# Choosing ScalarE or VectorE for PSUM copies by an estimate of both queues, packing the first chunk's score batches, and loading one x block by itself

## Chip, cores, metric

The kernel runs on one core of a Trainium2 chip. The metric is the device time of one execution in microseconds; the median of several executions is quoted, of "fast" runs alone. Ratios are computed as the mean time of one kernel's fast runs over that of the other's fast runs of the same rounds, so they are not quite the ratio of the medians that stand beside them.

## The reference

A layer normalisation feeds two branches, and the input is added to their sum:

```python
xn = layernorm(x)                        # S = 2048 rows, D = 512, bf16
qkv = xn @ wqkv                          # 32 heads of 16
scores = q @ k.T * 16**-0.5              # a query sees itself and the 255 keys before it
attn = softmax(masked scores) @ v @ wo
glu = ((xn @ w_gate) * (xn @ w_up)) @ w_down     # F = 1792
out = x + attn + glu
```

## The kernel before

The kernel works on four chunks of 512 rows. For each chunk and each group `c` of 8 heads it makes batches of scores, one exponential per batch, masks, and a values product. The dense matmuls (projections, gate, up, down, output) are "fillers" that are put between the batches by a count of cost units, one unit being about one 512-column matmul. The order of instructions on each engine is fixed when the program is built.

First, a chunk gets its tiles, and GpSimd writes the constants that V needs (ones in columns 16 and 17 of each head, which later give the softmax sums):

```python
def new_chunk(self, T):
    ...                                   # Q, K, Ko, V, VS tiles
    nc.gpsimd.memset(self.heads(self.V[T])[:, :, :, 16:18], 1.0)
    nc.gpsimd.memset(self.V[T][:, VW - 16:], 0.0)
    nc.gpsimd.memset(self.VS[T][:, SW - 16:], 0.0)
```

The copies out of PSUM, the memory (in banks) that TensorE writes its results to. V always goes to ScalarE and fills columns 0 to 15 of each head. K, Q and the gate go to ScalarE only when 11 units have passed since the last score batch (`act_free`), otherwise to VectorE:

```python
def proj_v(self, t, ks=range(4)):
    ...                                   # 4 matmuls into one PSUM bank
    nc.scalar.activation(out=self.heads(self.V[T])[:, b]...[:, :, :, 0:16], in_=ps..., func=ACT.Copy)

# in gate(); proj_qk() is alike
    if self.act_free:
        nc.scalar.activation(out=self.gsb[:], in_=ps[:], func=ACT.Copy)
    else:
        nc.vector.tensor_copy(out=self.gsb[:], in_=ps[:])
```

A batch of scores. There is one score tile of four banks (`bufs=1`), so the next batch can start only when the exponential has read the last one. GpSimd then cuts the far edge of the window with "triangles", two for each place:

```python
def scores(self, T, c, pieces):
    S = self.s_tiles.tile([128, 4, 512], F32, tag="S", name="S")
    ...                                   # 16 or 24 packed matmuls (32x64 tiles of the array)
    nc.scalar.activation(out=P[:, :, 0:col], in_=S[:, :, 0:col], func=ACT.Exp, scale=0.25)
    for at in self.places(pieces, 4):
        for half in (slice(0, 64), slice(64, 128)):
            self.triangle(P[half, :, at:at + 64], False)      # gpsimd.affine_select
```

```python
def project(T):
    add(0, lambda: self.new_chunk(T))
    for b in range(4):
        for ks in halves:
            add(2, lambda t=4 * T + b, ks=ks: self.proj_v(t, ks), self.first[T, 0])
    add(0, lambda: self.swap_halves(T, self.nc.sync), self.first[T, 0])
    ...                                   # Q and K projections
```

All other PSUM tiles, dense products and values sums alike, share a ring of four banks (`ps_m`).

The softmax here doesn't subtract the row's maximum and nothing guards it: scores larger than these inputs give would overflow.

## Time and profile before

| | before |
|---|---|
| median time | 269.14 us (3 runs; 268.98 us over the 4 runs known later) |
| span in the profile | 267.5 us |
| TensorE busy | 258.4 us (97%) |
| VectorE, ScalarE, GpSimd busy | 181.7, 170.6, 113.8 us |

The page of the kernel before gives busy time and share for each engine, and further down the chain that ended last, by engine:

```profile
span 267.5 us, 8861 instructions
...
PE 258.4 (97%) x3860; PEld 119.1 (45%) x3882; DVE 181.7 (68%) x352; ACT 170.6 (64%) x132; POOL 113.8 (43%) x281
...
PE 88%; DVE 7%; issue 1%; DMA 1%; ACT 1%; SPq 0%; POOL 0%; DVEq 0%; POOLq 0%
```

TensorE (PE) is busy nearly always and holds 88% of the chain. Busy time of matmuls can hide stalls, because the recorded ends are modelled. The starts are safer: count the dense matmuls between two score batches, allow 0.216 us for each, 0.45 us for the batch and, where a values sum falls between, 0.97 us (first chunk) or 1.27 us (later), and compare with the distance of the two batches' starts. (22 matmul records are missing from this trace, 3860 against 3882 weight loads.) What a distance has above its allowance is called a hole below. In this kernel all distances fit within 0.1 us but three, which hold 0.18, 0.31 and 0.15 us more.

The timeline of the kernel before, at the start (start us, duration us, engine, line, what; in brackets the idle time before it and who ended it):

```profile
2.86 0.69 DVE L148 BATCH_NORM_STATS2 st<-x 128x6 f32<-128x512 bf16 x1 [1.02 <-DMA x<-in_A_x_dram]
...
4.80 0.70 DVE L148 BATCH_NORM_STATS2 st<-x 128x6 f32<-128x512 bf16 x1 [0.84 <-DMA x<-in_A_x_dram]
...
14.43 0.28 PE L261 MATMUL S<-Q,K 16*64 16x192 bf16 x4
```

The second block's statistics wait for the load of three blocks at once, and the first scores come at 14.43 us.

### The profile page before, as it was taken

What the parts mean: (1) busy time and instruction counts of PE and PEld (TensorE: products, weight loads), DVE (VectorE), ACT (ScalarE), POOL (GpSimd) and SP (SyncE); (2) the same over time, 40 slices, a digit from 0 to 9 for tenths busy, and PEclk for the clock granted to TensorE, in tenths of its full rate; (3) what the DMA queues carried; (4) which work ended last, traced back from release to release, by engine and by line L of the source; (5) the groups of instructions that cost most, each with busy time, mean ns of one, the idle gap of its engine ahead of it and who ended that gap; (6) DMA issues with size and microseconds to landing.
All of it is one profiled execution on the core that took longest, in us unless ns stands there. A gap on an engine that the chain in (4) does not pass through costs nothing.

```text
span 267.5 us, 8861 instructions
## 1 busy us (share of the span) xinstructions
PE 258.4 (97%) x3860; PEld 119.1 (45%) x3882; DVE 181.7 (68%) x352; ACT 170.6 (64%) x132; POOL 113.8 (43%) x281
## 2 busy tenths in 40 slices
PE   6899999999999999999999999999999999999994
PEld 6444434444444444444444444444444444434453
DVE  4377898958756859676674868857762575978251
ACT  2675658696556776769656676668765667665500
POOL 5215333422674533345556433545444353443500
PEclk9999999999999999999999999999999999999999
DMA  6999911120023000001014100000200010000002
GB/s 205 373 358 334 250 22 22 23 47 0 4 61 81 20 2 4 2 2 44 5 23 97 43 0 5 0 4 2 44 5 20 26 39 2 2 0 2 4 2 81
DMA packets 19336, 15.13 MB, mean 57 GB/s; under 512 B 7264, under 2 KB 19296, under 8 KB 19296
## 3 DMA queue, kind: packets, MB, share of 16 engines
q1 hardware_dynamic: 18464, 14.09, 18.1%
q8 instruction: 30, 0.49, 0.7%
q10 hardware_dynamic: 832, 0.46, 0.6%
q14 instruction: 10, 0.08, 0.1%
HBM read 9.70 MB, written 2.10 MB: 44 GB/s over the span
## 4 chain that ended last, share of the span: by engine, by line
PE 88%; DVE 7%; issue 1%; DMA 1%; ACT 1%; SPq 0%; POOL 0%; DVEq 0%; POOLq 0%
PE up L359 17%; PE gp L345 17%; PE psd L378 16%; PE qkp L212 11%; PE S L261 9%; PE acc L316 6%; PE psd L384 5%; PE vp L200 4%; PE L L378 2%; DMA x<-in_A_x_dram 1%; DVE hT L363 1%; DVE st L148 1%; DVE at L322 1%; DVE gsb L353 1%; DVE xn L168 1%
## 5 line engine op out<-in xcount | busy, mean ns | idle before, releaser
L268 ACT ACTIVATE P<-S 128x2048 bf16<-128x2048 f32 x76 | 141.0, 1855 | 57.4 <-PE S L261 49.9
L137 POOL TENSOR_SCALAR_AFFINE_SELECT P<-P 64x256 bf16<-64x256 bf16 x224 | 97.3, 434 | 128.9 <-ACT P L268 118.2
L345 PE MATMUL gp<-xnT,Wg 128*128 128x512 bf16 x224 | 60.0, 380 | 0.1
L359 PE MATMUL up<-xnT,Wu 128*128 128x512 bf16 x224 | 59.6, 380 | 0.0
L378 PE MATMUL psd<-Wd,hT 128*128 128x512 bf16 (+1 forms) x198 | 48.7, 368 | 1.4 <-issue 1.3
L363 DVE TENSOR_TENSOR hT<-up,gsb 128x512 bf16<-128x512 f32 x56 | 38.4, 686 | 16.0 <-PE up L359 14.4
L289 DVE TENSOR_TENSOR P<-P,diag 128x512 bf16<-128x512 bf16 (+1 forms) x76 | 30.6, 404 | 10.4 <-ACT P L268 10.4
L322 DVE STREAM_TRANSPOSE at<-acc 128x512 f32<-128x512 f32 x30 | 19.7, 695 | 19.7 <-PE acc L316 19.7
L378 PEld LDWEIGHTS <-hT 128*128 128x128 bf16 x238 | 21.6, 98 | 25.3 <-issue 2.6
L359 PEld LDWEIGHTS <-Wu 128*128 128x128 bf16 x224 | 20.4, 98 | 25.3 <-issue 2.5
L345 PEld LDWEIGHTS <-Wg 128*128 128x128 bf16 x224 | 20.3, 98 | 25.5 <-issue 2.7
L261 PE MATMUL S<-Q,K 16*64 16x320 bf16 (+1 forms) x720 | 31.2, 260 | 0.4
L261 PE MATMUL S<-Q,Ko 32*64 32x320 bf16 (+1 forms) x720 | 31.1, 260 | 0.0
L212 PE MATMUL qkp<-xnT,Wqkv 128*128 128x512 bf16 x128 | 30.0, 380 | 0.0
L261 PEld LDWEIGHTS <-K 16*64 16x64 bf16 x720 | 12.2, 103 | 32.2 <-issue 32.2
L353 DVE CAST gsb<-gp 128x512 bf16<-128x512 f32 x36 | 24.5, 681 | 2.6 <-PE gp L345 1.3
L351 ACT ACTIVATE gsb<-gp 128x512 bf16<-128x512 f32 x20 | 11.9, 597 | 11.8 <-PE gp L345 11.1
L316 PE MATMUL acc<-P,VS 64*32 64x320 bf16 (+4 forms) x672 | 18.9, 254 | 0.0
L316 PE MATMUL acc<-P,V 64*32 64x320 bf16 (+4 forms) x672 | 18.4, 254 | 0.1
L212 PEld LDWEIGHTS <-Wqkv 128*128 128x128 bf16 x128 | 11.7, 98 | 14.5 <-issue 1.4
L384 PE MATMUL psd<-Wo,OT 128*128 128x512 bf16 (+1 forms) x55 | 15.5, 368 | 0.6 <-issue 0.6
L316 PEld LDWEIGHTS <-V 64*32 64x32 bf16 x720 | 14.5, 90 | 2.8 <-issue 2.4
(55 smaller groups left out, 194.1 us busy)
## 6 DMA issues: line engine op xcount, KB each, us to landing
Wg<-in_B_w_gate_dram SPq DMA_DIRECT2D x2, 896.0 KB, 10.4
Wu<-in_B_w_up_dram SPq DMA_DIRECT2D x2, 896.0 KB, 13.0
Wd<-in_B_w_down_dram SPq DMA_DIRECT2D x1, 1792.0 KB, 17.3
out_dram<-y SPq DMA_DIRECT2D x14, 128.0 KB, 1.8
Wqkv<-in_A_wqkv_dram SPq DMA_DIRECT2D x3, 512.0 KB, 6.4
x<-in_A_x_dram SPq DMA_DIRECT2D x1, 1024.0 KB, 10.9
VS<-V SPq DMA_DIRECT2D x6, 144.0 KB, 2.6
x<-in_A_x_dram SPq DMA_DIRECT2D x1, 512.0 KB, 11.4
```

The lines of the kernel that those rows point to most:

```text
L137: nc.gpsimd.affine_select(out=v, in_=v, pattern=pattern + [[1 if diag else -1, 64]], compare_op=ALU.is_ge if diag else ALU.is_gt, fill=0.0 ...
L212: nc.tensor.matmul(ps[:], lhsT=self.Wqkv[:, k, lo:lo + 128], rhs=self.xnT[T][:, :, k, :], start=(k == 0), stop=(k == 3))
L261: nc.tensor.matmul(S[64 * par:64 * par + 64, e, col:col + n], lhsT=(self.Ko if par else self.K)[U][rows, c, keys], rhs=self.Q[T][rows, c, ...
L268: nc.scalar.activation(out=P[:, :, 0:col], in_=S[:, :, 0:col], func=ACT.Exp, scale=0.25)
L289: self.nc.vector.tensor_tensor(out=v, in0=v, op=ALU.min, in1=self.diag.unsqueeze(1).unsqueeze(1).to_broadcast([128, 4, n, 64]))
L316: nc.tensor.matmul(accs[par][32 * e:32 * e + 32, q:q + n], lhsT=v, rhs=P[rows, e, col:col + n], start=(i == 0), stop=(i == len(todo) - 1), ...
L345: nc.tensor.matmul(ps[:], lhsT=self.Wg[:, k, 128 * f:128 * f + 128], rhs=self.xnT[T][:, :, k, :], start=(k == 0), stop=(k == 3))
L353: nc.vector.tensor_copy(out=self.gsb[:], in_=ps[:])
L359: nc.tensor.matmul(ps[:], lhsT=self.Wu[:, k, 128 * f:128 * f + 128], rhs=self.xnT[T][:, :, k, :], start=(k == 0), stop=(k == 3))
L363: nc.vector.tensor_tensor(out=self.hT[T][:, f, :], in0=ps[:], in1=self.gsb[:], op=ALU.mult)
L378: nc.tensor.matmul(ps, lhsT=self.hT[T][:, f, 128 * b:128 * b + 128], rhs=self.Wd[:, f, c0:c1], start=(f == 0), stop=False)
L384: self.nc.tensor.matmul(ps, lhsT=self.OT[T][:, c, 128 * b:128 * b + 128], rhs=self.Wo[:, c, c0:c1], start=False, stop=(c == 3))
```

## The change

The intent is to keep both copying engines' queues short, to save one score batch, and to start earlier:

- Every copy goes to the engine that an estimate says will finish it first. The estimate books, in cost units, what has been given to ScalarE and VectorE.
- The first chunk's 16 batches (four of them with 384 columns) become 15 of 512, some shared by two head groups. The cost constants that place the work go from 1.85 and 5.5 to 1.9 and 6.0.
- x is loaded as blocks 0, 1 and 2 to 3 instead of 0 and 1 to 3.
- At the end one store moves from ScalarE to VectorE, and the identity matmul that added x for it goes.

```diff
+REST = (((0, *SIX), (1, *SIX), (0, *FOUR)), ((1, *FOUR), (2, *FOUR)), ((2, *SIX), (3, *SIX), (3, *FOUR)))
+SCORES, VALUES = 1.9, 6.0
+COPY = dict(act=2.8, dve=3.2)
+EXP, MASK, HALF, SUMS, DIVIDE, TURN, STATS = 8.7, 1.9, 1.7, 4.2, 8.2, 6.1, 4.2
@@ loads
-        for lo, hi in ((0, 1), (1, 4)):
+        for lo, hi in ((0, 1), (1, 2), (2, 4)):
@@ copies
+    def book(self, engine, took, ready=0):
+        self.free[engine] = max(self.free[engine], self.now, ready) + took
+    def copy(self, out, in_, engine=None):
+        if engine is None:
+            engine = min(COPY, key=lambda e: max(self.free[e], self.now) + COPY[e])
+        self.book(engine, COPY[engine])
+        if engine == "act":
+            nc.scalar.activation(out=out, in_=in_, func=ACT.Copy)
+        else:
+            nc.vector.tensor_copy(out=out, in_=in_)
@@ proj_v (proj_qk and gate alike)
-        nc.scalar.activation(out=self.heads(self.V[T])[:, b]..., in_=ps..., func=ACT.Copy)
+        self.copy(self.heads(self.V[T])[:, b]..., ps..., engine)
@@ batches
+            out += [tuple((c, *p) for p in pieces) for pieces in (LATER if T else SHARED)]
+            if T == 0 and c < 3:
+                out.append(REST[c])
@@ tail
-            if b in (1, 3):
-                add(1, lambda b=b: self.add_x(T, b, 0 if b == 1 else 1))
+        add(1, lambda: self.add_x(T, 3, 1))
-            self.store(T, b, on_act=(b == 1))
+            self.store(T, b)
```

More of the change, by code (lines that the diff above doesn't have):

```diff
@@ L18 @@
 SW = 4 * 16 * 18 + 16
-FIRST = (((5, 5, 7), (0, 0, 4)), ((3, 3, 5), (1, 1, 5)),
-         ((3, 6, 7), (7, 7, 7), (2, 2, 6)), ((4, 4, 7), (6, 6, 7)))
+SHARED = ((5, 5, 7), (0, 0, 4)), ((3, 3, 5), (1, 1, 5)), ((3, 6, 7), (7, 7, 7), (2, 2, 6))
+FOUR, SIX = (4, 4, 7), (6, 6, 7)
 LATER = (((-2, 0, 2), (0, 0, 4)), ((5, 5, 7), (1, 1, 5)), ((-3, 0, 1), (7, 7, 7), (3, 3, 7)),
          ((-4, 0, 0), (6, 6, 7), (2, 2, 6)), ((-1, 0, 3), (4, 4, 7)))
-ACT_FREE = 11
+REST = (((0, *SIX), (1, *SIX), (0, *FOUR)), ((1, *FOUR), (2, *FOUR)), ((2, *SIX), (3, *SIX), (3, *FOUR)))
+SCORES, VALUES = 1.9, 6.0
+COPY = dict(act=2.8, dve=3.2)
+EXP, MASK, HALF, SUMS, DIVIDE, TURN, STATS = 8.7, 1.9, 1.7, 4.2, 8.2, 6.1, 4.2
 class Kernel:
@@ L107, in setup @@
         self.K, self.Ko, self.V, self.VS = {}, {}, {}, {}
-        self.strips, self.at = {}, {}
+        self.strips, self.parts, self.at = {}, {}, {}
     def new_chunk(self, T):
@@ L149, in norm_stats @@
         nc.vector.bn_aggr(out=self.mv[:, t % n, :], in_=st[:])
+        self.book("dve", STATS)
         self.stats[t] = [self.mv, t % n, None]
@@ L169, in norm_apply @@
                                 scalar2=rs[:, j:j + 1], op0=ALU.subtract, op1=ALU.mult)
+        self.book("dve", MASK)
         self.xns[t] = xn
@@ L193, in bank, with proj_v @@
         return self.cur
-    def proj_v(self, t, ks=range(4)):
+    def book(self, engine, took, ready=0):
+        self.free[engine] = max(self.free[engine], self.now, ready) + took
+    def copy(self, out, in_, engine=None):
+        nc = self.nc
+        if engine is None:
[5 more added lines that the diff above has]
+            nc.vector.tensor_copy(out=out, in_=in_)
+    def proj_v(self, t, ks=range(4), engine=None):
         nc = self.nc
@@ L203, in proj_v, with proj_qk @@
             return
-        nc.scalar.activation(out=self.heads(self.V[T])[:, b].rearrange("p (r g) d -> p r g d", r=2)[:, :, :, 0:16],
-                             in_=ps.rearrange("p (g r d) -> p r g d", g=16, r=2), func=ACT.Copy)
-    def proj_qk(self, T, c, is_k, ks=range(4), on_act=False):
+        self.copy(self.heads(self.V[T])[:, b].rearrange("p (r g) d -> p r g d", r=2)[:, :, :, 0:16],
+                  ps.rearrange("p (g r d) -> p r g d", g=16, r=2), engine)
+    def proj_qk(self, T, c, is_k, ks=range(4), engine=None):
         nc = self.nc
@@ L215, in proj_qk @@
             return
+        self.copy((self.K if is_k else self.Q)[T][:, c, :], ps[:], engine)
         if is_k:
-            if self.act_free:
-                nc.scalar.activation(out=self.K[T][:, c, :], in_=ps[:], func=ACT.Copy)
-            else:
-                nc.vector.tensor_copy(out=self.K[T][:, c, :], in_=ps[:])
             nc.vector.tensor_scalar(out=self.Ko[T][:, c, :], in0=self.K[T][:, c, :],
                                     scalar1=self.odd[:, 0:1], scalar2=None, op0=ALU.mult)
-        elif on_act or self.act_free:
-            nc.scalar.activation(out=self.Q[T][:, c, :], in_=ps[:], func=ACT.Copy)
-        else:
-            nc.vector.tensor_copy(out=self.Q[T][:, c, :], in_=ps[:])
+            self.book("dve", HALF)
     def first_chunk(self):
@@ L242, in first_chunk, with batches, scores @@
                 self.norm_transpose(b + 1, False)
-            self.proj_v(b)
-        self.proj_qk(0, 0, 1)
-        self.proj_qk(0, 0, 0, on_act=True)
+            self.proj_v(b, engine="act")
+        self.proj_qk(0, 0, 1, engine="dve")
+        self.proj_qk(0, 0, 0, engine="act")
         self.swap_halves(0, self.nc.scalar)
-        self.proj_qk(0, 1, 1)
-    def scores(self, T, c, pieces):
+        self.proj_qk(0, 1, 1, engine="dve")
+    def batches(self, T):
+        out = []
+        for c in range(4):
+            out += [tuple((c, *p) for p in pieces) for pieces in (LATER if T else SHARED)]
+            if T == 0 and c < 3:
+                out.append(REST[c])
+        return out
+    def scores(self, T, pieces):
         nc = self.nc
         S = self.s_tiles.tile([128, 4, 512], F32, tag="S", name="S")
+        P = self.ppool.tile([128, 4, 512], BF16, tag="P", name="P")
         col = 0
-        for m, q0, q1 in pieces:
+        for c, m, q0, q1 in pieces:
             U, j = divmod(8 * T + m, 8)
@@ L265, in scores @@
                                      skip_group_check=True)
+            self.parts.setdefault((T, c), []).append((P, col, m, q, n))
             col += n
-        P = self.ppool.tile([128, 4, 512], BF16, tag="P", name="P")
         nc.scalar.activation(out=P[:, :, 0:col], in_=S[:, :, 0:col], func=ACT.Exp, scale=0.25)
-        self.strips[(T, c, pieces)] = P
+        self.book("act", EXP)
+        self.masked = self.free["act"]
+        self.strips[(T, pieces)] = P
         for at in self.places(pieces, 4):
@@ L276, in places @@
         out, at = [], 0
-        for m, q0, q1 in pieces:
+        for _, m, q0, q1 in pieces:
             out += [at + 64 * (q - q0) for q in range(q0, q1 + 1) if q == m + far]
@@ L280, in places, with mask_diag @@
         return out
-    def mask_diag(self, T, c, pieces):
-        P = self.strips[(T, c, pieces)]
+    def mask_diag(self, T, pieces):
+        P = self.strips.pop((T, pieces))
         places = [at // 64 for at in self.places(pieces, 0)]
-        step = places[1] - places[0] if len(places) == 2 else 1
+        n = len(places)
+        step = places[1] - places[0] if n > 1 else 1
+        assert places == list(range(places[0], places[-1] + 1, step))
         v = P.rearrange("p e (b x) -> p e b x", x=64)[:, :, places[0]:places[-1] + 1:step, :]
-        n = len(places)
         self.nc.vector.tensor_tensor(out=v, in0=v, op=ALU.min,
                                      in1=self.diag.unsqueeze(1).unsqueeze(1).to_broadcast([128, 4, n, 64]))
+        self.book("dve", MASK, self.masked)
     def values(self, T, c, accs=None):
@@ L297, in values @@
             accs = [self.ps_m.tile([128, 512], F32, tag="M", name="acc") for _ in range(2)]
-        todo = []
-        for pieces in LATER if T else FIRST:
-            P, col = self.strips.pop((T, c, pieces)), 0
-            for m, q0, q1 in pieces:
-                todo.append((P, col, m, 64 * q0, 64 * (q1 - q0 + 1)))
-                col += 64 * (q1 - q0 + 1)
+        todo = self.parts.pop((T, c))
         for i, (P, col, m, q, n) in enumerate(todo):
@@ L322, in values @@
             nc.vector.transpose(out=at[:, par].rearrange("p b r -> p (b r)"), in_=accs[par][:])
+        self.book("dve", TURN)
         self.at[(T, c)] = at
@@ L335, in divide @@
                                 in1=rz.unsqueeze(3).to_broadcast([128, 2, 16, 16]), op=ALU.mult)
+        self.book("dve", DIVIDE)
         nc.vector.transpose(out=self.OT[T][:, c, :], in_=on.rearrange("p b r d -> p (b r d)"))
@@ L349, in gate @@
         self.gsb = self.work.tile([128, 512], BF16, tag="gsb", name="gsb")
-        if self.act_free:
-            nc.scalar.activation(out=self.gsb[:], in_=ps[:], func=ACT.Copy)
-        else:
-            nc.vector.tensor_copy(out=self.gsb[:], in_=ps[:])
+        self.copy(self.gsb[:], ps[:])
     def up(self, T, f, ks):
@@ L363, in up @@
         nc.vector.tensor_tensor(out=self.hT[T][:, f, :], in0=ps[:], in1=self.gsb[:], op=ALU.mult)
+        self.book("dve", COPY["dve"])
     def down(self, T, b, lo, hi):
@@ L402, in store @@
             nc.vector.tensor_tensor(out=y, in0=ps, in1=self.x[:, t, c0:c1], op=ALU.add)
+            self.book("dve", COPY["dve"])
         (nc.scalar if on_act else nc.sync).dma_start(out=self.out_d[128 * t:128 * t + 128, c0:c1], in_=y)
@@ L489, in run @@
         self.xns, self.stats, self.sums = {}, {}, {}
-        self.act_free = False
+        self.now, self.free = 0, dict(act=0, dve=0)
         self.setup()
@@ L496, in run @@
         for T in range(NCH):
-            for c in range(4):
-                self.first[T, c] = len(steps)
-                for pieces in LATER if T else FIRST:
+            for pieces in self.batches(T):
+                for c, *_ in pieces:
+                    self.first.setdefault((T, c), len(steps))
                     self.last[T, c] = len(steps)
-                    steps.append((T, c, pieces))
+                steps.append((T, pieces))
         due = {g: key for key, g in self.last.items()}
-        SCORES, VALUES = 1.85, 5.5
         self.beside = {}
@@ L506, in run @@
         total = sum(w[0] for w in work) - RESERVE + SCORES * len(steps) + VALUES * (len(due) - 1)
-        spent, n, scored = 0, 0, 0
+        spent, n = 0, 0
+        self.free = dict(act=0, dve=0)
         valued, ready = -1, -1
@@ L518, in fill @@
                     break
-                self.act_free = spent + cost - scored >= ACT_FREE
+                spent += cost
+                self.now = spent
                 f()
-                spent += cost
                 n += 1
@@ L527, in values @@
                 return False
+            spent += VALUES
+            self.now = spent
             self.values(*due[g])
-            spent += VALUES
             return True
@@ L539, in run @@
             valued = ready
+            spent += SCORES
+            self.now = spent
             self.scores(*s)
-            scored = spent
-            spent += SCORES
             upto = total * (g + 1) / len(steps)
```

## The prediction

> **What bounds the kernel now.** TensorE, almost without a hole. The page gives it 258.4 us busy of 267.5 (97%), granted clock 1.00; the chain of waits is 88% PE. "Busy" could hide stalls, so I read the distances between starts in the timeline: back-to-back 512-column matmuls start every 0.216 us in every stage, also where VectorE is fullest (9.75 of 10 us at 30 to 40 us, windows view). A score batch costs 0.45 us between the neighbouring matmuls, a values group 1.2 to 1.3 us, the same everywhere. From 8.4 to 263.8 us I find about 0.25 us of stall that is not a missing record (36.6 to 37.2 us). VectorE (182 us busy) and ScalarE (171 us) wait for PE far more than PE for them.
>
> **What the change does.**
> 1. Copies. In the built order ScalarE's gate copies go from 20 to 34, Q and K from 11 to 16, V from 16 to 10; VectorE's from 36 to 22, 21 to 16, 0 to 6. At 0.60 us (ScalarE) and 0.68 us (VectorE) VectorE loses about 8 us with the moved store, ScalarE gains 7. The Trainium skill ("TensorEngine Tiling (Array Packing)", PSUM Bottleneck) advises both engines for PSUM evacuation; but in this trace evacuation hardly stalls PE: worth 0.2 us. Risk: a copy behind a 1.88 us exponential keeps a bank, and the product waiting for it blocks VectorE. A gate bank is needed again some 2.6 us later, so I expect little of that.
> 2. First chunk: 15 batches of 512 columns for 12 of 512 and 4 of 384. Matmuls and columns stay; one entry and exit of the packed mode goes. The same page (Key Properties) says a mode switch drains TensorE; the trace has about 0.09 us before each batch. 16 batches take about 7.0 us, 15 about 6.75: 0.2 us of PE.
> 3. x block 1 alone. The start is critical: VectorE's second statistics begin at 4.80 us, when the 384 KB load lands (3.5 us after issue; the 128 KB load took 2.0). Alone, block 1 should land near 3.3 us and those statistics begin near 3.97 us. The chain from there (statistics, scale, transposes) moves 0.8 us earlier, up to PE at 8.43 us. Weight loads are issued about 0.45 us later (V's landed at 6.2 us, first use would be near 6.65), and the warm-up matmuls end at 5.67 us: I count 0.7 us.
> 4. Tail: one identity matmul (0.22 us) goes; its store moves to VectorE, which has room. Last bank to end unchanged (263.8 to 267.5 us).
>
> **Sum.** 0.7 + 0.2 + 0.2 + 0.2, all on the critical path, less perhaps 0.1 for new waits: about 1.3 us. From 269.1: **267.8 us**, range 267.0 to 269.0. Faster by over 2%: 0.01; within 2%: 0.97; slower by over 2%: 0.02.
>
> **What would show it.** Step 3: second statistics at about 4.0 us, first Q/K projection near 10.9 instead of 11.7 us. Step 2: 75 exponentials, all 128x2048, 0.45 us per batch. Step 1: VectorE busy near 174 us, ScalarE near 178, PE start distances still 0.216 us. Step 4: last matmul 1.2 to 1.5 us earlier, last bank to end about 3.5 us as before.
>
> **What would make it wrong.** If block 1 lands with the others, step 3 vanishes (near 268.5). If V's weights land late, it shrinks by up to 0.4. If copies behind exponentials hold banks, PE starts show holes in the gate stages and the result may be 269 or more.

## More of the kernel before

The experiments ran in three groups. The kernels of a group shared one chip and one set of runs of the kernel before.

The waits view of the kernel before reads: who waited for whom, total us, times, longest us.

```profile
ACT P L268 <- PE S L261: 49.9, 51, 1.8
...
ACT V L204 <- POOL V L118: 1.4, 1, 1.4
```

ScalarE's exponentials (P) wait for TensorE's scores. The second line is a small one and was not discussed in the prediction: once, a V copy on ScalarE waited 1.4 us for GpSimd to write V at L118, which is the memset of the ones. It cost TensorE 0.15 us.

```profile
116.10 1.47 PE L200 MATMUL vp<-Wqkv,xnT 128*128 128x512 bf16 x5
...
116.97 0.89 POOL L137 TENSOR_SCALAR_AFFINE_SELECT P<-P 64x256 bf16<-64x256 bf16 x2 [1.18 <-ACT P L268]
...
117.92 0.33 POOL L118 MEMSET V<- 128x256 bf16 x1
...
118.28 0.60 ACT L204 ACTIVATE V<-vp 128x512 bf16<-128x512 f32 x1 [1.38 <-POOL V L118]
...
118.78 1.87 ACT L268 ACTIVATE P<-S 128x2048 bf16<-128x2048 f32 x1
...
120.70 0.22 PE L261 MATMUL S<-Q,K 16*64 16x64 bf16 x4
```

GpSimd does two triangles, then the memset; one V copy waits for it, and ScalarE goes on to the next exponential, which ends just before TensorE wants the score tile again at 120.70 us.

## The result, and the profile after

| | before | after |
|---|---|---|
| median time | 268.98 us (4 runs) | 271.0 us (4 runs, 270.78 to 271.27) |
| span in the profile | 267.5 us | 269.1 us |
| first scores | 14.43 us | 13.91 us |
| VectorE, ScalarE busy | 181.7, 170.6 us | 175.5, 176.2 us |

The ratio is 1.0076, with a 95% interval of 1.0059 to 1.0094. The change makes the kernel 2.0 us slower where 1.3 us faster was forecast. The profiled runs differ by 1.97 us in time but by 1.6 us in span, the stretch that the trace covers. The rest goes with the built kernel more than with the single run: time less span is 1.67 to 1.79 us in all 29 executions of the kernel before beside the experiments, and 2.07 to 2.10 us in the four of the changed one. No trace shows where this 0.35 us is spent, and I don't explain it.

The page of the changed kernel:

```profile
span 269.1 us, 8894 instructions
...
PE 261.0 (97%) x3881; PEld 119.6 (44%) x3881; DVE 175.5 (65%) x339; ACT 176.2 (65%) x143; POOL 114.8 (43%) x281
...
PE 81%; issue 6%; POOL 5%; ACT 4%; DVE 1%; DMA 1%; POOLq 0%; ACTq 0%
```

The totals are as forecast, and they hide the loss: TensorE is still "97% busy". The chain tells more, because GpSimd (POOL) and ScalarE, which held 1% together before, now hold 9% of it. The waits view of the changed kernel names the links:

```profile
ACT V L211 <- POOL V L121: 4.8, 2, 2.4
...
PE S L285 <- ACT P L292: 2.1, 2, 1.2
...
PE qkp L232 <- ACT V L211: 0.8, 2, 0.6
```

Twice a V copy on ScalarE waits 2.4 us for the memset (L121 is the old L118); at the second place one on VectorE waits 1.6 us as well. Twice a score batch waits for an exponential, which never happened before. Twice a projection waits for a bank that a V copy has to empty. By the distances of score starts there are exactly two holes over 0.1 us in the whole run, 1.70 and 1.72 us, at the V projections of the third and the fourth chunk. The timeline of the changed kernel at the first of them:

```profile
117.00 1.91 POOL L140 TENSOR_SCALAR_AFFINE_SELECT P<-P 64x256 bf16<-64x256 bf16 x4 [2.15 <-ACT P L292]
...
118.34 1.04 PE L220 MATMUL vp<-Wqkv,xnT 128*128 128x512 bf16 x4
118.97 0.33 POOL L121 MEMSET V<- 128x256 bf16 x1
...
119.33 1.57 ACT L211 ACTIVATE V<-vp 128x512 bf16<-128x512 f32 x3 [2.39 <-POOL V L121]
119.49 0.69 DVE L213 CAST V<-vp 128x512 bf16<-128x512 f32 x1 [1.80 <-PE vp L220]
119.98 1.89 PE L232 MATMUL qkp<-xnT,Wqkv 128*128 128x512 bf16 x8 [0.59 <-ACT V L211]
...
120.78 1.90 ACT L292 ACTIVATE P<-S 128x2048 bf16<-128x2048 f32 x1
...
122.72 0.30 PE L285 MATMUL S<-Q,K 16*64 16x256 bf16 x4 [0.86 <-ACT P L292]
```

Read it from the top. GpSimd has four triangles to do, not two, so the memset of V comes at 118.97 us. ScalarE is idle for 2.39 us ahead of its V copies, then does three of them. Only then, at 120.78 us, comes the exponential of a batch whose last scores were issued by 118.1 us. TensorE stops twice: 0.77 us for a PSUM bank (118.34 plus four times 0.216 is 119.20, the next start is 119.98), and 0.92 us for the score tile. The second hole splits into 0.41 and 1.30 us.

The chain of waits in order of time for the same stretch says the same (start us, us, what):

```profile
115.06 1.89 ACT P L292
...
118.50 0.41 POOL P L140
...
118.97 0.34 POOL V L121
...
119.33 1.57 ACT V L211 x3
120.90 1.78 ACT P L292
```

The start, in the timeline of the changed kernel, moved as intended, though less:

```profile
3.03 0.69 DVE L151 BATCH_NORM_STATS2 st<-x 128x6 f32<-128x512 bf16 x1 [1.20 <-DMA x<-in_A_x_dram]
...
4.05 0.68 DVE L151 BATCH_NORM_STATS2 st<-x 128x6 f32<-128x512 bf16 x1
...
13.91 0.28 PE L285 MATMUL S<-Q,K 16*64 16x192 bf16 x4
```

From first to last score batch the kernel before takes 235.82 us for 847 dense matmuls and 75 intervals, the changed one 237.88 us for 845 and 74. The two holes (+3.42), the three small ones that are gone (-0.64), one batch fewer (-0.20, as e3 against e1 shows below) and two matmuls (-0.43; both belong to the down projection and moved behind the last scores) add up to +2.15 for the measured +2.06 us. The dropped identity isn't in this stretch: in the kernel before it ran at 253.85 us, after the last scores.

### The profile page after: what moved, and what is told of

It is laid out like the page before. It is cut to its first block, busy times and chain, and to the rows that moved or that the text cites. A ratio compares the mean times of both kernels' runs of the same rounds, so it can differ in the third digit from the quotient of the medians.

```text
span 269.1 us, 8894 instructions
## 1 busy us (share of the span) xinstructions
PE 261.0 (97%) x3881; PEld 119.6 (44%) x3881; DVE 175.5 (65%) x339; ACT 176.2 (65%) x143; POOL 114.8 (43%) x281
## 4 chain that ended last, share of the span: by engine, by line
PE 81%; issue 6%; POOL 5%; ACT 4%; DVE 1%; DMA 1%; POOLq 0%; ACTq 0%
PE psd L401 17%; PE gp L370 15%; PE up L381 15%; PE qkp L232 10%; PE S L285 9%; PE acc L339 6%; POOL P L140 5%; PE psd L407 5%; PE vp L220 3%; ACT P L292 3%; PE L L401 2%; ACT V L211 1%; DMA x<-in_A_x_dram 1%; DVE st L151 1%; PE L L407 1%
## 5 line engine op out<-in xcount | busy, mean ns | idle before, releaser
L370 PE MATMUL gp<-xnT,Wg 128*128 128x512 bf16 x224 | 58.9, 380 | 0.0
L401 PE MATMUL psd<-Wd,hT 128*128 128x512 bf16 (+1 forms) x210 | 51.8, 369 | 0.0
L316 DVE TENSOR_TENSOR P<-P,diag 128x512 bf16<-128x512 bf16 (+1 forms) x75 | 29.4, 392 | 10.4 <-ACT P L292 10.4
L285 PE MATMUL S<-Q,K 16*64 16x320 bf16 (+4 forms) x720 | 31.0, 260 | 2.1 <-ACT P L292 2.1
L285 PE MATMUL S<-Q,Ko 32*64 32x320 bf16 (+4 forms) x720 | 31.0, 260 | 0.0
L211 ACT ACTIVATE gsb<-gp 128x512 bf16<-128x512 f32 x34 | 20.0, 596 | 15.5 <-PE gp L370 13.5
L213 DVE CAST gsb<-gp 128x512 bf16<-128x512 f32 x22 | 15.2, 691 | 3.3 <-PE gp L370 2.0
L407 PE MATMUL psd<-Wo,OT 128*128 128x512 bf16 (+1 forms) x60 | 16.4, 369 | 0.0
```

What stands on the lines that cost most here:

```text
L211: nc.scalar.activation(out=out, in_=in_, func=ACT.Copy)
L285: nc.tensor.matmul(S[64 * par:64 * par + 64, e, col:col + n], lhsT=(self.Ko if par else self.K)[U][rows, c, keys], rhs=self.Q[T][rows, c, ...
L316: self.nc.vector.tensor_tensor(out=v, in0=v, op=ALU.min, in1=self.diag.unsqueeze(1).unsqueeze(1).to_broadcast([128, 4, n, 64]))
L370: nc.tensor.matmul(ps[:], lhsT=self.Wg[:, k, 128 * f:128 * f + 128], rhs=self.xnT[T][:, :, k, :], start=(k == 0), stop=(k == 3))
L401: nc.tensor.matmul(ps, lhsT=self.hT[T][:, f, 128 * b:128 * b + 128], rhs=self.Wd[:, f, c0:c1], start=(f == 0), stop=False)
L407: self.nc.tensor.matmul(ps, lhsT=self.OT[T][:, c, 128 * b:128 * b + 128], rhs=self.Wo[:, c, c0:c1], start=False, stop=(c == 3))
```

## The experiments

Theory A: the memset of V's ones stands in GpSimd's queue behind the triangles of a batch, and these wait for that batch's exponential. V copies wait for the memset. ScalarE works in the order of its program, so the next exponential stands behind the waiting V copies, and TensorE waits for it. What changed is only the place: `new_chunk` now falls behind the third batch of a group (four triangles) for the third and fourth chunk; before had it behind the second (two).

Rival B: the new copy rule loads ScalarE too much, and its copies delay the exponentials, memset or not. Rival C: packing the batches is itself the cause.

The Trainium skill says, on the page "TensorE: Matmul & The Clock Gate" (the opening table, "Engine queue depth"), that ScalarE, VectorE and GpSimd take their queues strictly first in, first out. The trace agrees: the exponential's scores were there 2.4 us before it started, and the engine was idle for part of that time.

### e1_early_memset

```diff
 def project(T):
-    add(0, lambda: self.new_chunk(T))
 def gu(T, between):
     for f in range(NF):
         ...
+        if f == 6 and T + 1 < NCH:
+            add(0, lambda: self.new_chunk(T + 1))
```

> The changed kernel, but each chunk's ones and zeros of V and VS are written on GpSimd half a chunk earlier (after the seventh feature of the gate stage); every other instruction keeps its place. Theory A (the two new stalls come from V's memset, which stands on GpSimd behind the four triangles of a score batch; the V copies wait for it, ScalarE's next exponential stands behind the V copies, and TensorE waits for that exponential): both stalls of 1.7 us vanish, so the time is the changed kernel's less 3.4 us, 1.4 us under before, near 267.6 us, ratio about 0.995; no wait of a V copy for GpSimd is left. Rival B (the new rule gives ScalarE too many copies and these delay the exponentials, memset or not): nothing changes, 2.0 us over before.

Measured: 267.59 us (6 runs) against 269.07 us for before (11 runs), ratio 0.9941 (0.9915 to 0.9967). No distance between score batches is over its allowance by 0.05 us any more. The timeline of this kernel at the same place:

```profile
116.40 1.08 ACT L211 ACTIVATE V<-vp 128x512 bf16<-128x512 f32 x2
116.57 1.91 POOL L140 TENSOR_SCALAR_AFFINE_SELECT P<-P 64x256 bf16<-64x256 bf16 x4 [2.15 <-ACT P L292]
...
117.66 0.60 ACT L211 ACTIVATE V<-vp 128x512 bf16<-128x512 f32 x1 [0.18 <-PE vp L220]
...
118.15 1.87 ACT L292 ACTIVATE P<-S 128x2048 bf16<-128x2048 f32 x1
...
120.61 0.30 PE L285 MATMUL S<-Q,K 16*64 16x256 bf16 x4
```

The same three V copies stand before the same exponential, and the same four triangles run at the same point of the program. The copies no longer wait, so the exponential starts at 118.15 us and the next scores have no wait. One line of the waits view goes against the expectation that no V copy waits for GpSimd: a copy on VectorE at 182.63 us is put down to a triangle (1.3 us). Its own product ended at about the same moment, there is no hole, and in e6 the same copy's wait (1.2 us) is put down to its product. Moving each later chunk's three memsets is worth 3.4 us, and this version beats both kernels. Theory A forecast 267.6 us; B forecast no change and falls.

### e2_old_copy_rule

```diff
-            engine = min(COPY, key=lambda e: max(self.free[e], self.now) + COPY[e])
+            engine = 'act' if self.act_free else 'dve'      # act_free: 11 units since the last scores
@@ V copies of the later chunks
-    self.proj_v(t, ks)
+    self.proj_v(t, ks, engine='act')
```

> The changed kernel with the copy rule of before (ScalarE only when 11 units have passed since the last scores, V copies all on ScalarE); packed batches, x loads, cost constants and tail stay changed. In the built order the memset of V for the third and fourth chunk still stands behind the triangles of the third batch (four of them), where before had it behind the second batch (two). Theory A: the stalls stay, 3 to 4 us of them, and the time is 1.5 to 2.8 us over before. Rival B (copy rule is the cause): the stalls go and the time is about 1 us under before.

Measured: 270.76 us (4 runs), ratio 1.0055 (1.0019 to 1.0091). The holes are 1.70 and 1.72 us, at the same two places and of the same size. The waits view of this kernel has the changed kernel's figures:

```profile
ACT V L211 <- POOL V L121: 4.8, 2, 2.4
...
PE S L285 <- ACT P L292: 2.1, 2, 1.2
```

Going back to the old rule takes nothing of the loss away, so B falls a second time, from the other side.

### e3_old_batches

```diff
-            out += [tuple((c, *p) for p in pieces) for pieces in (LATER if T else SHARED)]
-            if T == 0 and c < 3:
-                out.append(REST[c])
+            out += [tuple((c, *p) for p in pieces) for pieces in (LATER if T else (*SHARED, (FOUR, SIX)))]
```

> The changed kernel with the first chunk's scores in the 16 batches of before; new copy rule, x loads, constants and tail stay. In the built order the memset of V stands behind the second batch (two triangles) for the third chunk, as before has it, and behind the third batch (four) for the fourth chunk, as the changed kernel has it. Theory A: one stall of the two is left, near the fourth chunk's projection, about 1.7 us; with one batch more (0.25 to 0.45 us) the time is about 0.6 us over before. Rival B: both stalls stay, 2.3 us over before. Rival C (packing itself is the cause): both stalls go, 0.9 us under before.

Measured: 269.27 us (4 runs), ratio 1.0001 (0.997 to 1.0033). The third chunk's hole shrinks to the 0.15 us that before has, the fourth chunk's stays at 1.57 us. So the hole goes with the place of the memset, chunk by chunk, as the built order says; packing as such doesn't bring it (C falls). The time is 0.4 us under the forecast of 0.6 us over before. Most of that lies outside the span: time less span is 1.7 us here and 2.1 us in the changed kernel, from whose time I forecast. From first to last scores this trace takes 236.42 us and that of e1 takes 234.50; less the 1.72 us of holes, one batch more costs 0.20 us, where I had allowed 0.25 to 0.45.

### e4_x_split_alone

```diff
-        for lo, hi in ((0, 1), (1, 4)):
+        for lo, hi in ((0, 1), (1, 2), (2, 4)):
```

(in the kernel before)

> Before, with x block 1 loaded by itself and nothing else. The prediction on record counted 0.7 us for it; the trace of the changed kernel shows its first scores 0.52 us earlier (13.91 against 14.43 us), with the TensorE clock granted at 7.2 us instead of 6.0 us. If the late clock belongs to this change, 0.5 us faster than before; if it varies from run to run, 0.5 to 0.8 us.

Measured: 268.68 us (6 runs) against 269.07, ratio 0.9977 (0.9953 to 1.0002). The medians differ by 0.39 us, but the interval touches 1, so the gain is likely rather than proven by time alone. In the trace the second statistics start at 4.03 us, and the first scores at 13.81 us. V's weights land at 6.83 us instead of 6.22, and the first V projection starts at 6.96 us: that is the term that the prediction named and undercounted. In the nine traces with the split, V's weights land between 6.34 and 7.28 us. In seven of them the first V projection starts 0.13 to 0.14 us after that landing. The clock was granted at 5.2 us here, so the late clock of the changed kernel's profile doesn't belong to the split; it varies from run to run. One profile of each kernel is a coarse measure of the start: over all traces the first scores come at 13.48 to 14.26 us in the nine with the split, and at 14.04, 14.43 and 16.24 us in the three without.

### e5_v_copies_on_dve

```diff
-    self.proj_v(t, ks)                    # in project(), later chunks
+    self.proj_v(t, ks, engine='dve')
```

> The changed kernel with all V copies of the later chunks on VectorE; the memset of V still stands behind four triangles. Theory A splits each stall in two terms: TensorE waits for a bank that a V copy empties (0.77 and 0.41 us), and for the score tile, whose exponential stands behind the V copies on ScalarE (0.93 and 1.30 us). With no V copy on ScalarE the second term goes and the first stays: about 2.2 us under the changed kernel, so within 0.3 us of before, with holes of 0.4 to 0.8 us left and no score batch waiting for an exponential. If the bank alone matters (VectorE copies start as late), 2 us over before.

Measured: 268.69 us (4 runs) against 269.24, ratio 0.9977 (0.995 to 1.0004); 2.3 us under the changed kernel by the medians of the two groups. The holes are 0.81 and 0.45 us. The timeline of this kernel at the first:

```profile
118.20 1.88 ACT L292 ACTIVATE P<-S 128x2048 bf16<-128x2048 f32 x1 [1.61 <-PE S L285]
...
118.92 1.89 DVE L213 CAST V<-vp 128x512 bf16<-128x512 f32 x3 [2.02 <-POOL V L121]
119.67 1.89 PE L232 MATMUL qkp<-xnT,Wqkv 128*128 128x512 bf16 x8 [0.63 <-DVE V L213]
```

VectorE now waits for the memset, as ScalarE did, and TensorE still waits for the bank. But the exponential isn't behind the copies, starts at once, and no score batch waits. This splits the 3.4 us: 1.2 to 1.3 us come from PSUM banks held by copies that cannot start, about 2.2 us from exponentials behind those copies.

### e6_memset_after_copies

```diff
 def new_chunk(self, T):
-    nc.gpsimd.memset(...)                 # ones and zeros of V, VS
+    if T == 0:
+        self.ones(0)                      # the same three memsets
@@ project(T), after the four V projections
+    add(0, lambda: self.ones(T), self.first[T, 0])
     add(0, lambda: self.swap_halves(T, self.nc.sync), self.first[T, 0])
```

> The changed kernel with the memsets of V and VS of the later chunks issued after that chunk's V copies; the columns are disjoint (16 and 17 of each head against 0 to 15), so the result is the same, and no V copy waits for GpSimd. GpSimd does the same work at about the same place. Theory A: it is only the order that costs, both stalls go, 267.6 us as with the early memset. If GpSimd's work in that stretch were the cost[...], the stalls would stay, 2 us over before.

Measured: 267.17 us (4 runs) against 269.24, ratio 0.9921 (0.9894 to 0.9948), correct, no holes. (The medians put this kernel 0.4 us under e1, but the spans agree, 265.4 to 265.6 us here against 265.2 to 266.4 us; the 0.4 us is again time outside the span.) GpSimd does the same triangles and memsets, the memsets later: that of the third chunk comes at 122.39 us, after its last V copy, which ends at 119.80 us. So it is not GpSimd's work that costs but who must wait for it, and nobody needs to: the copies and the memset write different columns of the tile.

### e7_constants_into_before

```diff
-        SCORES, VALUES = 1.85, 5.5
+        SCORES, VALUES = 1.9, 6.0
```

(in the kernel before)

> Before, with only the two cost constants that place the work changed (1.85 to 1.9 and 5.5 to 6.0). By the built order the memset of V for the fourth chunk now stands behind the third score batch (four triangles) instead of the second (two); the third chunk's stays behind the second. Copies, batches and loads are those of before. Theory A: a stall of about 1.6 us appears at the fourth chunk's projection and none at the third's beyond 0.15 us: 1.6 us over before. Rival B (copy rule) and C (packing): same as before.

Measured: 270.73 us (4 runs) against 269.24, ratio 1.0054 (1.0026 to 1.0081). Two cost constants alone make the kernel before 1.5 us slower. The hole is at the fourth chunk, 2.22 us long instead of the 1.6 us expected; the third chunk's stays at 0.15. This trace starts its scores 0.39 us earlier than the first trace of before did (14.04 us), which hides some of it. The waits view of this kernel:

```profile
ACT V L204 <- POOL V L118: 3.9, 2, 2.5
...
PE qkp L212 <- ACT V L204: 1.1, 1, 1.1
...
PE S L261 <- ACT P L268: 0.9, 1, 0.9
```

The V copies wait for the memset up to 2.5 us (1.4 us in the kernel before), and the pair of TensorE waits of the changed kernel is there, once, in a kernel with the old copies, old batches and old loads. Before's own order has three V copies ahead of an exponential at the fourth chunk too, without a hole, because there the memset came at 181.19 us, 1.9 us ahead of the first copy.

### e8_early_memset_in_before

The diff of e1, applied to the kernel before.

> Control: before, with the memset of V half a chunk earlier and nothing else. In before a V copy waits 1.4 us for it once, and TensorE loses 0.15 us there: 0.1 to 0.2 us faster, not more. If the early memset were worth something by itself beyond the stalls of the changed kernel, it would show here as 1 us or more.

Measured: 269.05 us (5 runs) against 269.24, ratio 0.9989 (0.9955 to 1.0022): the same, as a control should be. The 0.15 us hole is gone from the trace. The early memset pays only where the wait exists. The profiled run was the longest of its five (270.83 us), which is of use below.

### e9_early_memset_old_copies and e10_early_memset_again

The diffs of e1 and e2 together, and e1 once more beside it.

> The early memset with the copy rule of before; packed batches, x loads, constants, tail stay changed. It asks what the new copy rule is worth once its stalls are gone. The run with the old copy rule had no other hole than the two stalls, so theory A: within 0.3 us of the early memset with the new rule, about 1.4 us under before, both without holes; the new rule is then worth nothing. If the new rule is worth the 0.2 us of the prediction or the 0.5 us of holes that before has at 36 and 43 us, this one is that much slower than the early memset beside it.

> The early memset in the changed kernel again, on the same chip as the one with the old copy rule: 1.4 us under before, as in its first run.

Measured: 267.45 us (5 runs) with the old copy rule, 267.66 us (6 runs) with the new one, before 268.97; ratios 0.9935 (0.9915 to 0.9954) and 0.9942 (0.9922 to 0.9963). The two can't be told apart. With the new rule VectorE is busy 175.7 us and ScalarE 176.2 us (e1), with the old one 178.4 and 172.9 us; TensorE has no hole with the new rule and one of 0.11 us with the old. The rule that gave the change its name is worth nothing here.

## Why the prediction was wrong

- **What bounds the kernel.** Right. TensorE is the limit, its cost per matmul and per batch is the same in all traces, and without the stalls the time came out at 267.6 us, 1.5 us under before, for a forecast gain of 1.3. That this sum comes so near is partly luck: the prediction had read 0.25 us of stall in before where the distances hold 0.64 us, and about 0.3 us of time outside the span took some of the gain back.
- **Step 1, copies: here it failed.** The prediction said "less perhaps 0.1 for new waits"; the runs show 3.4 us. It looked for the risk in "a copy behind a 1.88 us exponential", that is in how long a ready copy stands in its queue. What happened was the reverse, an exponential behind copies that were not ready. They weren't because of GpSimd, which the change doesn't mention, and which neither the change's estimate of queues nor my own had in it. The copy rule isn't even the cause (e2, e9). The place of a zero-cost item in the program is: with the old batches the third chunk's hole is gone (e3), and the two cost constants alone bring the fourth chunk's into before (e7). I had the built order to compare and counted its copies, but I did not follow what each V copy waits for. The line "ACT V L204 <- POOL V L118" in before's waits was the warning: a wait of 1.4 us that cost TensorE 0.15 us shows a dependency with no slack left.
- **Step 1, gain.** Forecast 0.2 us. Before's small holes (0.49 us at 36 and 43 us) are gone, but e2 and e9, with the old rule, lack them too; so does e3, with the new rule and old batches, while e4 and e7, with the old rule and old batches, keep them. So the new rule or the new batches each seem to be enough, and in the changed kernel the rule adds nothing.
- **Step 2, packed batches.** Right: 0.20 us (e3 against e1, from traces), 75 exponentials, all of 2048 columns. What it cost by moving `new_chunk` was not seen.
- **Step 3, x block 1 alone.** Right mechanism, over-sized. Statistics at 4.05 us as forecast, first scores 0.52 us earlier in the profile and 0.39 us of median time alone (e4) for 0.7 us forecast. The later weights take their part in most traces. In the changed kernel's own profile the late clock does: TensorE's record of the full clock begins at 7.2 us, and the first transposes and the first matmul of the V projection ran at about half speed (starts 0.11 us apart where e4 has 0.06, and 0.39 where it has 0.22).
- **Step 4, tail.** One matmul less, as counted; not measured by itself. From the last matmul's start to the end it takes 3.75 us in before's trace and 3.6 us in the changed kernel's.

What stays open: 0.09 us of the budget between first and last scores, and the time outside the span, which goes mostly with the built kernel: 1.7 us in before, e2, e3, e4, e6 and e7, 2.0 to 2.2 us in the changed kernel, e1, e5 and e10 (e1 and e10 are one kernel on two chips), 1.8 to 2.1 us in e8 and e9. So a difference of 0.4 us between two medians here need not stand in any trace.

## What to carry to other kernels

When a change moves work about, list for each moved instruction everything that it waits for, also from engines that the change doesn't touch, and check in the built order what stands ahead of those producers; a wait that is nearly hidden today is a stall after a small shift. On engines that work in order, a copy that isn't ready delays everything behind it, so a rule that picks an engine by queue length must also know when the operand is ready. Constant fills belong far ahead of their use, or behind the writes with which they merely share a tile.

## What the Trainium skill lacked or had wrong

- "TensorE: Matmul & The Clock Gate" (opening table) has the strict order of the ScalarE, VectorE and GpSimd queues, but no page that I read joins it to copies: "TensorEngine Tiling (Array Packing)", PSUM Bottleneck, advises to use both engines for PSUM evacuation. Here a better balance (175.7 and 176.2 us busy instead of 178.4 and 172.9) was worth nothing (267.66 against 267.45 us), while one copy queue blocked by another engine's memset cost 3.4 us.
- "TensorEngine Tiling (Array Packing)", Key Properties, says that a mode switch drains TensorE and gives no cost. Here a packed score batch between dense matmuls costs 0.45 us, about 0.09 us of it before its first matmul, and one batch fewer with the same matmuls and columns saves 0.20 us.
- "TensorE: Matmul & The Clock Gate", Part 1, says that the activity window of about 3.4 us is free-running, so that the transition varies by about half a microsecond, and advises against fitting a count of slow matmuls. (Its own count of 6, 11 or 14 of them in one kernel already points to more.) The traces show a larger spread than half a microsecond: with the first warm-up matmul at 1.42 or 1.43 us in all twelve, the full clock was granted between 4.25 and 7.22 us in eleven and at 10.60 us in one. The first eleven spread over 3.0 us, which a free-running window of 3.4 us leaves room for; the window itself is not shown by these runs. That one (the profiled run of e8, at 270.83 us against its kernel's median of 269.05) has the x load landing at 5.33 us, and TensorE idle for 0.96 us between the warm-up matmuls and the first transposes; its V projection still runs at half speed, as the lines below show. Of 42 runs without the split x load, 6 were over 1.2 us above the median of their group, of 43 with it none. Only one of these six was traced, so the link between the two is likely, not shown.

The timeline of the early memset in before (e8) at the start; four V matmuls take 1.91 us from the first start to the last end, where the changed kernel's fully clocked ones take 1.03:

```profile
5.35 0.70 DVE L148 BATCH_NORM_STATS2 st<-x 128x6 f32<-128x512 bf16 x1 [1.26 <-DMA x<-in_A_x_dram]
...
6.62 0.61 PE L186 MATMUL xTp<-ident,xn 128*128 128x128 bf16 x4 [0.96 <-DVE xn L168]
...
8.21 1.91 PE L200 MATMUL vp<-Wqkv,xnT 128*128 128x512 bf16 x4
```
